# Copying transposed tokens out of PSUM: the order in which the elements of one copy are walked

## The chip, the cores and the metric

The kernel runs on one core of one Trainium2 chip. The metric is the device time of an execution in microseconds (us). In the profile PE is TensorE (PEld its weight loads), DVE is VectorE, ACT is ScalarE, POOL is GpSimd, which here issues the loads. Lnnn is a source line.

## The reference

A sliding-window attention (window 64) feeds a soft mixture of experts.

```python
batch, n_heads, seq, head_dim = (8, 8, 576, 64)      # q, k, v, float32
N, D, E, S_per_e, F = (4608, 512, 8, 4, 1024)        # phi, w1, w2, float32

mask = (rel >= 0) & (rel < 64)
attn = softmax(where(mask, q @ k.T / 8, -1e9))       # per head
x = (attn @ v) as [4608, 512]
logits = x @ phi                                     # 32 slots
slot_input = softmax(logits, over tokens).T @ x
slot_out[e] = relu(slot_input[e] @ w1[e]) @ w2[e]
out = softmax(logits, over slots) @ slot_out
```

## The kernel before

The attention is done in 16 units (8 batches, two halves of four heads each). In a load of q, k or v a partition holds 9 consecutive tokens of one head ("t", T = 9), and the 64 groups of a head ("g") lie on 64 partitions, so that a partition's piece is 9 x 64 elements of one head in a row. The price is that a transpose of one token slice gives columns in the order (h, g) for a single t, and the copy out of PSUM has to put the tokens back into their sequence, where token number = 9 g + t.

```python
def t1(src, dst, on_vector):
    for t0, n in ((0, 5), (5, 4)):
        tr = ps.tile([128, 8, 128], FP16, name="tr", tag="tr")     # PSUM, two buffers
        for j in range(n):
            for x in range(2):
                nc.tensor.transpose(tr[64 * x:64 * x + 64, j, :],
                                    src[:, x, 64 * (t0 + j):64 * (t0 + j) + 64], ident[:, :])
        o = dst.rearrange("p h (g t) -> p t h g", t=T)[:, t0:t0 + n]
        i = tr[:, 0:n, :].rearrange("p t (h g) -> p t h g", h=2)
        if on_vector:
            nc.vector.tensor_copy(out=o, in_=i)      # kT
        else:
            nc.scalar.copy(out=o, in_=i)             # qT, vT

# the order of one unit, cut to the calls (the scheduler moves some of them)
for u in range(nu):
    issue_loads(u)             # q, k, v of unit u + 2, and one weight tile of 1 MB
    for j in range(3):
        stage_t2(u, j)         # transposes windows of vT through "tr", copies to vw (DVE)
        stage_s(u, j)          # scores, exp (ACT), mask (DVE)
        stage_t1(u + 1, j)     # j = 0, 1, 2: t1 of q, k, v of the next unit
        stage_av(*pend)        # attn @ v of the step before, normalised (DVE)
        # ... and one piece of the slot work of a finished batch, also through "tr"
# ... then the experts and the output
```

So each unit has six of these copies: two (5 tokens = 640 elements per partition, 4 tokens = 512) for each of qT and vT on ACT and kT on DVE.

The softmax here doesn't subtract the row's maximum and nothing guards it: scores larger than these inputs give would overflow.

## Time and profile before

| | before |
|---|---|
| time, median of 2 runs | 416.34 us |
| attention stage (16 units of about 21.7 us) | to about 347 us |
| tail (last slot work, experts, output) | about 68 us |
| the six copies, busy time over all units | 252.9 us |

The first lines of the profile's page: busy time and share of the span, then the span in 40 slices of 10.4 us, where a digit is the busy share in tenths, PEclk the granted TensorE clock in tenths, DMA the share of the DMA engines and GB/s what they moved.

```profile
span 414.8 us, 6919 instructions
PE 208.4 (50%) x3028; PEld 152.7 (37%) x3028; DVE 204.5 (49%) x420; ACT 221.8 (53%) x160; POOL 51.7 (12%) x77
...
PEclk9999999999999999999999999999999999889655
DMA  8993997969693979596423324240003300000798
GB/s 110 191 180 49 137 153 105 184 84 184 89 187 48 188 124 177 89 173 112 58 28 43 46 30 57 30 54 5 1 2 53 50 2 2 2 0 2 287 377 246
```

No engine is busy for much over half the time, so the kernel looks like a chain of handoffs. The list of groups by shape shows the copies (count, busy us, mean ns of one, then the idle time before them):

```profile
L143 ACT COPY qT<-tr 128x640 f16<-128x640 f16 x16 | 47.5, 2971 | 15.2 <-PE tr L136 15.2
L143 ACT COPY qT<-tr 128x512 f16<-128x512 f16 x16 | 40.0, 2497 | 0.0
...
L143 ACT COPY vT_103<-tr 128x640 f16<-128x640 f16 x8 | 23.8, 2971 | 43.8 <-PE tr L136 43.8
...
L141 DVE COPY kT_102<-tr 128x640 f16<-128x640 f16 x8 | 23.7, 2961 | 9.9 <-PE tr L136 9.9
...
L167 PEld LDWEIGHTS <-vT_103 128*128 128x128 f16 x144 | 14.8, 137 | 40.8 <-issue 25.5 <-ACT vT_103 L143 14.7
```

A copy takes 2.96 to 2.98 us for 640 elements on both engines: something that they share may set the pace. The timeline shows where such copies stand; the columns are start, duration, engine, line, operation, and in brackets the idle time before it and what ended it. This is one unit, cut to the chain:

```profile
192.55 1.03 PE L167 MATMUL tr<-ident,vT_103 128*128 128x128 f16 x8 [1.50 <-ACT vT_103 L143]
...
194.31 2.98 ACT L143 COPY qT<-tr 128x640 f16<-128x640 f16 x1 [0.78 <-PE tr L136]
...
198.01 2.44 ACT L143 COPY qT<-tr 128x512 f16<-128x512 f16 x1
...
200.50 1.01 PE L167 MATMUL tr<-ident,vT_103 128*128 128x128 f16 x8 [1.69 <-ACT qT L143]
...
202.23 5.22 DVE L141 COPY kT_111<-tr 128x640 f16<-128x640 f16 x2
...
209.23 5.24 ACT L143 COPY vT_112<-tr 128x640 f16<-128x640 f16 x2 [6.41 <-PE tr L136]
...
214.52 1.03 PE L167 MATMUL tr<-ident,vT_112 128*128 128x128 f16 x8 [1.35 <-ACT vT_112 L143]
```

Between the first and the last line lie 22 us, of which the six copies take 15.9: q, then k, then v, with PE waiting for each, because the next transposes need a "tr" buffer that a copy still reads, or the copied tile itself.

### The profile page before, as it was taken

To read this page: it belongs to the slowest core of one execution; us is meant where nothing else is said; L and a number is where in the kernel's file an instruction comes from. 1 tells how busy PE (TensorE), PEld (TensorE's weight loads), DVE (VectorE), ACT (ScalarE), POOL (GpSimd) and SP (SyncE) were. 2 spreads that over 40 slices of the span, in tenths; PEclk is the share of its full clock that TensorE was granted. 3 is DMA by queue.
4 is the path that set the end of the run, shared out by engine and by line. 5 is a ranking of instruction groups with operands and counts; after the bars stand their busy time and mean duration, and the time that the engine had idled before them with its cause. 6 is when DMAs were issued, how large, how long until landed. Compare 5 with 4: busy or idle time off the path is not lost. (4 is left out here: it accounts for less than half of the span.)

```text
span 414.8 us, 6919 instructions
## 1 busy us (share of the span) xinstructions
PE 208.4 (50%) x3028; PEld 152.7 (37%) x3028; DVE 204.5 (49%) x420; ACT 221.8 (53%) x160; POOL 51.7 (12%) x77
## 2 busy tenths in 40 slices
PE   1444445454544545445464544546445455799710
PEld 1333334343433434334344333435334344533100
DVE  0554545546373727273745455464637375511920
ACT  5665666574738291928374665647382916111920
POOL 8311202112121211211001010010001000000000
PEclk9999999999999999999999999999999999889655
DMA  8993997969693979596423324240003300000798
GB/s 110 191 180 49 137 153 105 184 84 184 89 187 48 188 124 177 89 173 112 58 28 43 46 30 57 30 54 5 1 2 53 50 2 2 2 0 2 287 377 246
DMA packets 31069, 40.83 MB, mean 98 GB/s; under 512 B 1856, under 2 KB 22336, under 8 KB 31040
## 3 DMA queue, kind: packets, MB, share of 16 engines
q0 software_dynamic: 26144, 30.97, 49.0%
q1 hardware_dynamic: 4896, 9.44, 6.6%
q8 instruction: 23, 0.38, 0.4%
q14 instruction: 6, 0.05, 0.0%
HBM read 61.93 MB, written 9.44 MB: 172 GB/s over the span
## 5 line engine op out<-in xcount | busy, mean ns | idle before, releaser
L143 ACT COPY qT<-tr 128x640 f16<-128x640 f16 (+1 forms) x32 | 85.5, 2734 | 15.2 <-PE tr L136 15.2
L143 ACT COPY vT_112<-tr 128x640 f16<-128x640 f16 (+1 forms) x16 | 42.0, 2845 | 52.4 <-PE tr L136 52.4
L143 ACT COPY vT_103<-tr 128x640 f16<-128x640 f16 (+1 forms) x16 | 41.9, 2832 | 44.5 <-PE tr L136 44.5
L187 ACT ACTIVATE pm<-sc 128x1024 f16<-128x1024 f32 (+1 forms) x48 | 46.4, 967 | 33.0 <-issue 28.1
L141 DVE COPY kT_102<-tr 128x640 f16<-128x640 f16 (+1 forms) x16 | 41.7, 2794 | 9.9 <-PE tr L136 9.9
L141 DVE COPY kT_111<-tr 128x640 f16<-128x640 f16 (+1 forms) x16 | 41.7, 2790 | 2.2 <-PE tr L136 2.2
L167 PE MATMUL tr<-ident,vT_112 128*128 128x128 f16 x144 | 19.4, 307 | 45.6 <-ACT vT_112 L143 20.8
L169 DVE COPY vw_104<-tr 128x512 f16<-128x512 f16 (+1 forms) x48 | 15.0, 353 | 47.9 <-PE tr L167 47.9
L167 PE MATMUL tr<-ident,vT_103 128*128 128x128 f16 x144 | 19.9, 306 | 37.1 <-ACT vT_103 L143 13.4
L249 PE MATMUL tr<-ident,x_bp 128*128 128x128 f16 x144 | 18.6, 305 | 38.5 <-DVE kT_111 L141 16.6
L191 DVE TENSOR_TENSOR pm<-pm,mask_98 128x512 f16<-128x512 f16 (+1 forms) x96 | 29.8, 349 | 15.7 <-ACT pm L187 15.6
L167 PEld LDWEIGHTS <-vT_112 128*128 128x128 f16 x144 | 14.4, 135 | 48.0 <-issue 25.0
L169 DVE COPY vw_113<-tr 128x512 f16<-128x512 f16 (+1 forms) x48 | 15.2, 352 | 30.0 <-PE tr L167 30.0
L249 PEld LDWEIGHTS <-x_bp 128*128 128x128 f16 x144 | 15.0, 135 | 40.8 <-issue 40.5
L214 PEld LDWEIGHTS <-pm 128*64 128x64 f16 x576 | 28.1, 158 | 4.7 <-issue 2.4
L167 PEld LDWEIGHTS <-vT_103 128*128 128x128 f16 x144 | 14.8, 137 | 40.8 <-issue 25.5
L136 PE MATMUL tr<-ident,qn 128*64 128x128 f16 x288 | 21.3, 313 | 12.5 <-ACT qT L143 7.0
L136 PE MATMUL tr<-ident,vn 128*64 128x128 f16 x288 | 22.2, 311 | 10.6 <-DVE kT_102 L141 2.4
L251 DVE COPY xT<-tr 128x1024 f16<-128x1024 f16 (+1 forms) x20 | 13.7, 686 | 26.6 <-PE tr L249 26.6
L136 PE MATMUL tr<-ident,kn 128*64 128x128 f16 x288 | 21.4, 312 | 7.3 <-ACT qT L143 7.2
L220 DVE RECIPROCAL rc<-av 128x8 f32<-128x8 f32 x32 | 9.2, 287 | 27.0 <-PE av L214 27.0
L222 DVE TENSOR_TENSOR x_bp<-av,rc 128x512 f16<-128x512 f32 x32 | 21.8, 682 | 0.5
(78 smaller groups left out, 323.2 us busy)
## 6 DMA issues: line engine op xcount, KB each, us to landing
out_dram<-ob SPq DMA_DIRECT2D x18, 512.0 KB, 5.5
w1s<-in_moe_w_dram POOLq DMA_DIRECT2D x8, 1024.0 KB, 10.5
w2s<-in_moe_w_dram POOLq DMA_DIRECT2D x7, 1024.0 KB, 10.6
qn<-in_q_dram POOLq DMA_DIRECT2D x16, 288.0 KB, 4.3
kn<-in_k_dram POOLq DMA_DIRECT2D x16, 288.0 KB, 5.1
vn<-in_v_dram POOLq DMA_DIRECT2D x16, 288.0 KB, 5.3
w2l<-in_moe_w_dram POOLq DMA_DIRECT2D x2, 512.0 KB, 7.3
phi_sb<-in_moe_phi_dram POOLq DMA_DIRECT2D x1, 32.0 KB, 5.6
```

Source lines behind the costliest of these rows:

```text
L136: nc.tensor.transpose(tr[64 * x:64 * x + 64, j, :], src[:, x, 64 * (t0 + j):64 * (t0 + j) + 64], ident[:, :])
L141: nc.vector.tensor_copy(out=o, in_=i)
L143: nc.scalar.copy(out=o, in_=i)
L167: nc.tensor.transpose(tr[:, h * n + w, :], st["vT"][:, h, 64 * i:64 * i + 128], ident[:, :])
L169: nc.vector.tensor_copy(out=st["vw"][:, wins[0]:wins[0] + n, h::2, 0:64], in_=tr[:, h * n:h * n + n, :].rearrange("p w (x d) -> p w x d", ...
L187: nc.scalar.activation(pm[:, :, 0:2 * n, :], sc[:, :, 0:128 * n].rearrange("p x (w q) -> p x w q", q=64), AF.Exp, scale=scale)
L191: nc.vector.tensor_tensor(out=pm[:, x, 0:2 * n, :], in0=pm[:, x, 0:2 * n, :], in1=mask0[:, :].unsqueeze(1).broadcast_to([128, 2 * n, 64]), ...
L214: nc.tensor.matmul(av[r0:r0 + 64, kk, 65 * (w // 2):65 * (w // 2) + 65], pm[:, x, h * n + w, :], st["vw"][:, i, kk, 0:65], start=True, sto ...
L220: nc.vector.reciprocal(rc[:, :, :], avv[:, :, :, 64])
L222: nc.vector.tensor_tensor(out=xb[:, c0:c0 + 2, 256 * half:256 * half + 256].rearrange("p c (k d) -> p k c d", d=64), in0=avv[:, :, :, 0:64 ...
L249: nc.tensor.transpose(tr[:, 4 * n + kk, :], xb[:, c, 128 * kk:128 * kk + 128], ident[:, :])
L251: nc.vector.tensor_copy(out=xT[:, 0:4 * len(ch), :], in_=tr[:, 0:4 * len(ch), :])
```

## The change

The intent: let the copy write SBUF in rising order (the tokens of one group innermost) and read PSUM with a stride instead. No instruction is added or removed.

```diff
-            o = dst.rearrange("p h (g t) -> p t h g", t=T)[:, t0:t0 + n]
-            i = tr[:, 0:n, :].rearrange("p t (h g) -> p t h g", h=2)
+            o = dst.rearrange("p h (g t) -> p h g t", t=T)[:, :, :, t0:t0 + n]
+            i = tr[:, 0:n, :].rearrange("p t (h g) -> p h g t", h=2)
```

Before, the write steps 9 elements (18 bytes) and the read is contiguous. After, the write makes runs of 5 (or 4) elements of every 9, and the read steps 128 elements (256 bytes).

## The prediction

> **What bounds the kernel.** No engine is full: the first table has PE at 50%, DVE 49%, ACT 53% of 414.8 us. By the timeline the attention stage (to about 347 us) runs 16 units of 21.7 us, each a chain of handoffs through two PSUM buffers "tr": transposes of v windows (1.0 us), token transposes (0.8), the copies that this change touches, then the next transposes, which wait for a buffer or a copied tile. In the unit from 192.5 to 214.5 us: qT 2.98 + 2.44 on ACT, kT 5.22 on DVE, vT 5.24 on ACT: 15.9 of 22 us, nearly all exposed. The list of waits agrees. From 347 us on, experts and output take 68 us, untouched.
>
> **Why a copy is slow.** A 128x640 copy takes 2.97 us on both engines: 4.3 ns per element after some 0.2 us fixed. It reads contiguously; its write steps 18 bytes[...].[...] plain copies on DVE (xT, 128x1024) take 0.75 us, and the hT cast, which writes runs of 4 contiguous fp16, takes 0.218 us for 64 elements[...]. So 4.3 ns seems to be paid per line, hidden when a line gets four elements.
>
> **What the change does.** Instructions, data and order of work stay. Writes become runs of 5 (or 4) elements, 10 (8) bytes of every 18, in rising order: about 144 lines instead of 640. The read now steps 256 bytes of PSUM.[...] I take reads as nearly free. Estimate for a copy:[...] 0.75 to 1.2, say 1.0 us (0.9 for 512). Six copies cost 5.8 us instead of 15.9.
>
> **On the critical path.** With shorter copies in the timeline's order a unit takes about 12.6 us. That alone would give 416 - 16 x 9.1 = 270 us. A second limit comes up: DMA. In 10 to 160 us its engines are 84 to 89% busy, as nearly all weights load between units 3 and 11. Before unit 12 can be transposed, 26 MB must land; at 157 GB/s (that stretch over its busy share) to 190 (best slices) this takes 138 to 168 us; compute alone needs 152. Sum: about 165 us to unit 12, 58 for the rest, 68 tail.
>
> **Predicted: 290 us, 8 in 10 between 260 and 345.** Faster by over 2%: 0.87; within 2%: 0.08; slower: 0.05.
>
> **What would show it.** Copies qT, kT, vT at 0.75 to 1.2 us in the list of groups; ACT busy falling from 222 to near 110 us, DVE from 205 to near 145; units near 13 us late in the attention stage, longer before; DMA share above 0.95 until about 165 us; transposes waiting for q/k/v loads; the tail unchanged.
>
> **What would make it wrong.** If a strided PSUM read costs like a strided SBUF write, nothing changes.[...] If writes are penalised per 4- or 8-byte word, copies take up to 1.9 us: about 355.

The sum behind the size of a copy came to 0.75 to 1.2 us, entered as 1.0 us for 640 elements and 0.9 for 512, 5.8 us for the six. These sizes, and the total of 291 us built on them (12.6 us a unit; 165 + 58 + 68), are estimates, and so is "reads as nearly free", which no view of the kernel before shows. The 0.2 us fixed is close to what an operation on 4 elements per partition takes on DVE in the trace before (L228, 178 ns). "Line" means 16 bytes of a partition's SBUF: an assumption when this was written, measured later by the first set of copies (write steps of 4, 8 and 9 elements: 1290, 2420 and 2391 ns).

## The result

The kernel after takes 244.97 us (median of 2 runs, 244.91 to 245.03) against 416.34 us; the ratio is 0.588, interval 0.586 to 0.591. Ratios here are the mean time of one kernel's runs over the mean of the other's of the same rounds, so they are not quite the ratio of the quoted medians. The direction was right, the size was not: the time lies below the predicted range of 260 to 345 us.

| | before | after |
|---|---|---|
| time | 416.34 us | 244.97 us |
| six copies, busy time over all units | 252.9 us | 70.2 us |
| ACT busy / DVE busy | 221.8 / 204.5 us | 100.9 / 147.1 us |
| from the start of the slot normalisation (L351) to the end | 54.9 us | 54.1 us |

(The copies' sums are the busy time of lines 141 and 143, without the one table load of 1.3 us on line 143. Adding the groups by shape would give 267.6 and 72.3 us, but the record of a 512 copy often starts before that of the 640 copy has ended, and such time counts once. The last row is the span less the start of that instruction in the chain that ended last, 359.94 and 188.92 us.) The page of the kernel after, slices of 6.1 us:

```profile
span 243.0 us, 6919 instructions
PE 168.3 (69%) x3028; PEld 121.0 (50%) x3028; DVE 147.1 (61%) x420; ACT 100.9 (42%) x160; POOL 51.7 (21%) x77
...
PEclk9999999999996555965756657999996599965555
DMA  5999999999999999999999999006500000079996
GB/s 86 159 192 211 206 207 210 208 209 211 208 212 205 209 208 208 211 206 211 207 209 208 207 206 163 2 3 94 84 3 0 3 0 4 0 270 378 379 374 154
```

Two things are new: the DMA engines are full from the second slice to the 25th (about 150 us), from the fourth to the 24th at 205 to 212 GB/s, and after that they are nearly idle, while attention goes on until 189 us. The groups by shape:

```profile
L143 ACT COPY qT<-tr 128x640 f16<-128x640 f16 x16 | 12.1, 758 | 10.5 <-PE tr L136 10.4
L143 ACT COPY qT<-tr 128x512 f16<-128x512 f16 x16 | 11.8, 735 | 0.0
...
L143 ACT COPY vT_103<-tr 128x640 f16<-128x640 f16 x8 | 6.1, 757 | 25.0 <-PE tr L136 25.0
...
L141 DVE COPY kT_102<-tr 128x640 f16<-128x640 f16 x8 | 6.6, 821 | 7.6 <-PE tr L136 7.4
...
L167 PEld LDWEIGHTS <-vT_103 128*128 128x128 f16 x144 | 11.2, 112 | 6.4 <-ACT vT_103 L143 2.7 <-issue 1.9
```

A copy of 640 now takes 0.76 us on ACT and 0.82 on DVE. The list of waits (us in total, times, longest) has a kind that before had only at the very start:

```profile
PE tr L136 <- DMA vn<-in_v_dram: 17.6, 5, 4.7
...
PEld L136 <- DMA kn<-in_k_dram: 3.7, 5, 1.9
```

And the timeline of one late unit, when the loads are done, cut like the one of before:

```profile
158.01 0.62 PE L167 MATMUL tr<-ident,vT_112 128*128 128x128 f16 x8 [0.17 <-ACT vT_112 L143]
...
159.07 0.76 ACT L143 COPY qT<-tr 128x640 f16<-128x640 f16 x1 [0.22 <-PE tr L136]
...
160.62 0.73 ACT L143 COPY qT<-tr 128x512 f16<-128x512 f16 x1
...
161.41 0.61 PE L167 MATMUL tr<-ident,vT_112 128*128 128x128 f16 x8 [0.33 <-ACT qT L143]
...
162.79 1.45 DVE L141 COPY kT_102<-tr 128x640 f16<-128x640 f16 x2
...
165.37 1.53 ACT L143 COPY vT_103<-tr 128x640 f16<-128x640 f16 x2 [2.26 <-PE tr L136]
```

The vT copies of successive units start at 156.43 and 165.37 us: a unit takes 9 us. Note the first line: eight transposes that took 1.03 us before take 0.62 here, though nothing about them was changed.

### The profile page after: what moved, and what is told of

It reads as the page before. It is cut to its first block, busy times and chain, and to the rows that moved or that the text cites. A ratio compares the mean times of both kernels' runs of the same rounds, so it can differ in the third digit from the quotient of the medians.

```text
span 243.0 us, 6919 instructions
## 1 busy us (share of the span) xinstructions
PE 168.3 (69%) x3028; PEld 121.0 (50%) x3028; DVE 147.1 (61%) x420; ACT 100.9 (42%) x160; POOL 51.7 (21%) x77
## 5 line engine op out<-in xcount | busy, mean ns | idle before, releaser
L187 ACT ACTIVATE pm<-sc 128x1024 f16<-128x1024 f32 (+1 forms) x48 | 39.1, 814 | 25.0 <-issue 18.9
L143 ACT COPY qT<-tr 128x640 f16<-128x640 f16 (+1 forms) x32 | 23.4, 746 | 10.5 <-PE tr L136 10.4
L143 ACT COPY vT_112<-tr 128x640 f16<-128x640 f16 (+1 forms) x16 | 11.8, 739 | 32.3 <-PE tr L136 32.1
L136 PEld LDWEIGHTS <-vn 128*64 128x64 f16 x288 | 12.7, 131 | 21.2 <-DMA vn<-in_v_dram 18.8
L143 ACT COPY vT_103<-tr 128x640 f16<-128x640 f16 (+1 forms) x16 | 11.7, 739 | 27.0 <-PE tr L136 25.5
L61 POOL DMA_DIRECT2D vn<-in_v_dram x16 | 11.4, 715 | 33.0 <-DMA w2s<-in_moe_w_dram 8.4
L167 PE MATMUL tr<-ident,vT_112 128*128 128x128 f16 x144 | 14.7, 251 | 5.2 <-ACT vT_112 L143 2.6
L167 PE MATMUL tr<-ident,vT_103 128*128 128x128 f16 x144 | 15.2, 250 | 3.7 <-ACT vT_103 L143 1.5
L136 PEld LDWEIGHTS <-qn 128*64 128x64 f16 x288 | 11.8, 132 | 10.1 <-DMA qn<-in_q_dram 5.6
L141 DVE COPY kT_102<-tr 128x640 f16<-128x640 f16 (+1 forms) x16 | 11.7, 768 | 7.6 <-PE tr L136 7.4
L61 POOL DMA_DIRECT2D kn<-in_k_dram x16 | 11.4, 714 | 21.1 <-PE tr L136 6.9
L214 PE MATMUL av<-vw_113,pm 128*64 128x65 f16 x288 | 14.3, 216 | 1.3 <-DVE x_bp L229 0.8
```

The costliest lines, as they stand in the source:

```text
L61: nc.gpsimd.dma_start(out=t, in_=src[b, 4 * half:4 * half + 4].rearrange("(x h) (g t) d -> (h g) x (t d)", x=2, h=2, t=T))
L136: nc.tensor.transpose(tr[64 * x:64 * x + 64, j, :], src[:, x, 64 * (t0 + j):64 * (t0 + j) + 64], ident[:, :])
L167: nc.tensor.transpose(tr[:, h * n + w, :], st["vT"][:, h, 64 * i:64 * i + 128], ident[:, :])
L187: nc.scalar.activation(pm[:, :, 0:2 * n, :], sc[:, :, 0:128 * n].rearrange("p x (w q) -> p x w q", q=64), AF.Exp, scale=scale)
L214: nc.tensor.matmul(av[r0:r0 + 64, kk, 65 * (w // 2):65 * (w // 2) + 65], pm[:, x, h * n + w, :], st["vw"][:, i, kk, 0:65], start=True, sto ...
```

## The experiments

My theory after the result had three parts: (1) the copies stand one after the other on the chain, so what each saves shows in the time; (2) a copy is slow because of how its write falls on SBUF, and a strided PSUM read is free; (3) after the change the loads hold the first 150 us. Rivals are named with each run. Times of the kernel before in the same rounds were 415.4 to 416.2 us (medians).

### Half the change: k_only and qv_only

The new order for kT alone (DVE), or for qT and vT alone (ACT):

```diff
+            if on_vector:          # k_only;   qv_only: if not on_vector
                 o = ... "p h g t" ...
+            else:
+                 o = ... "p t h g" ...
```

> Only the kT copies (DVE) get the new order. Chain theory (all six copies of a unit stand one after the other on the chain): saves 5.2 - 1.5 = 3.7 us in each of 16 units, about 59 us, 350 to 360 us. Rival (ACT, the busiest engine, is what bounds, DVE's copies are beside the path): stays within 2% of 416.

> Only the qT and vT copies (ACT) get the new order. Chain theory: saves 10.7 - 3.0 = 7.7 us per unit, 123 us, about 285 to 300 us. Rival (ACT bounds): nearly the whole gain, 245 to 255 us.

k_only took 359.25 us (ratio 0.864, interval 0.862 to 0.866), qv_only 300.35 us (0.722, 0.720 to 0.725). The first is inside the chain theory's range, the second 0.4 us above it. The rival (only ACT bounds) is out: k_only leaves ACT's busy time at 221.7 us and still saves 56 us. The kT copies save 83.4 - 24.1 = 59.3 us of busy time and qT and vT 169.4 - 46.9 = 122.5; the runs saved 56.2 and 115.1, so 95 and 94% of each is exposed. (In k_only PE's window transposes stayed as long as before, 306 ns on average; in qv_only they got shorter, 274 ns, so part of its gain may be PE's.)

### What makes a copy slow: bench, bench2 and bench3

Copies of single forms were appended to the end of the kernel after, each three times on ACT and on DVE, out of a PSUM tile into SBUF. They were single looks of unknown state (349.5, 290.6 and 262.0 us with the added copies); within each form the three copies differ by at most 5 ns, but for one that ranged from 1289 to 1337, and no time of the whole is used. Such a line, with its form (the write takes one element of every 9, the read is contiguous):

```diff
+            eng(out=X[:, 0:4608].rearrange("p (c s) -> p c s", s=9)[:, :, 0], in_=s4)
```

> The kernel after, with copies of single forms appended at its end, three of each on ACT and on DVE (512 or 640 fp16 per partition). Line theory (a write pays about 4.2 ns for every new 16-byte SBUF line, hidden when the line gets 4 or more elements; a strided PSUM read is free): write step 2 elements[...] as cheap as step 1, about 0.6 to 0.7 us; step 4 (2 per line) about 1.3 us; step 8, 9 about 2.4 us; runs of 2 of every 9 about 1.3 us, runs of 4 or 5 about 0.65 to 0.8; strided PSUM read into a contiguous write the same as contiguous to contiguous[...]; from SBUF with write step 9 also about 2.4. Rival 1 (any write whose inner step is not 1 is slow, whatever the line): steps 2 and 4 cost 2.4 us like step 9. Rival 2 (what is slow belongs to reading PSUM in long contiguous runs or to PSUM at all): step 9 from SBUF is fast.

The first set, in the groups by shape (L429 contiguous to contiguous, L433 write step 9, L437 strided read with contiguous write, L439 the form after, L440 the form before, L441 write step 9 from SBUF):

```profile
L440 ACT COPY X<-P 128x640 f16<-128x640 f16 x3 | 8.8, 2949 | 0.1
...
L441 ACT COPY X<-Y 128x512 f16<-128x512 f16 x3 | 7.3, 2422 | 0.1
...
L433 ACT COPY X<-P 128x512 f16<-128x512 f16 x3 | 7.2, 2391 | 0.1
...
L441 DVE COPY X<-Y 128x512 f16<-128x512 f16 x3 | 3.9, 1287 | 0.1
...
L439 ACT COPY X<-P 128x640 f16<-128x640 f16 x3 | 2.3, 752 | 0.1
...
L437 ACT COPY X<-P 128x512 f16<-128x512 f16 x3 | 1.8, 586 | 0.1
```

The strided PSUM read (L437) takes 586 ns, to the nanosecond what contiguous to contiguous takes on ACT (also 586): there it is free. On DVE it takes 691 against 423 ns. Of its strided reads, 640 elements took 825 ns and 512 took 691: 1.05 ns per element and 155 ns fixed. With the same fixed part the contiguous form takes 0.52 ns per element, so DVE is twice as fast there; the change loses that, and it does not matter beside 2.4 us. Rival 2 is out on ACT: from SBUF, step 9 is as slow as from PSUM (2422 and 2391 ns). Rival 1 is out: step 2 took 727 ns and step 4 1290, not 2400. The 16 bytes of a line show as well: from step 4 to step 8 the time rises from 1290 to 2420 ns, and at step 9 it is no longer (2391). But runs of 2 of every 9 took 1090 ns where the line rule wanted 1.3 us, so the rule got a second test.

> More single forms at the end of the kernel after, to test the rule that the first set fitted: time = 0.16 us + the larger of the elements' own rate (0.83 ns on ACT) and 4.4 ns for each time the write enters another 16-byte line. Expected on ACT: step 7, 512 elements: 0.16 + 512 x 14/16 x 4.4 = 2.1 us; step 12, 384 elements: 1.85 us; step 18, 256 elements: 1.29 us; runs of 2 of every 8, 256 runs: 1.29 us (the runs of 2 of every 9 took 1.09, less than the rule's 1.3 to 1.4, so here it may fail); runs of 2 of every 18: 1.29 us; runs of 4 of every 8, 128 lines: 0.73 us. Out of order: single elements put alternately into two contiguous halves: 2.4 us if only one line is kept open, about 0.6 if several are; runs of 4 put alternately into two halves: 0.73 us against 0.6.

```profile
L435 ACT COPY X<-P 128x512 f16<-128x512 f16 x3 | 7.2, 2412 | 0.1
...
L432 ACT COPY X<-P 128x512 f16<-128x512 f16 x3 | 1.8, 607 | 0.1
```

L432 is the runs of 2 of every 8, each in a 16-byte line of its own: 607 ns, not 1290. L435 writes single elements alternately into two contiguous halves: 2412 ns, although each line is filled in the end. The other forms of whole words missed it as well: pairs of every 18 took 612 ns instead of 1290, and runs of 4, of every 8 or in two halves, 586 and 585 instead of 730. So my rule "4.4 ns per new line" failed. What separates the cheap forms (585 to 612 ns) from the dear one (2412) is that a pair that starts at an even element fills one aligned 4-byte word, and a lone fp16 element does not. A third set tested that:

> The second set refuted the rule of 4.4 ns per new line: aligned runs of 2 or 4, each in its own line, cost nothing extra. New rule: what costs 4.4 ns is a lone 2-byte element, half of an aligned 4-byte word, once for each line entered with one; whole words are free wherever they fall. Expected on ACT under it: pairs that start at an odd element, 2 of every 8 (two half words each, 256 lines): 1.29 us; runs of 3 of every 8 (a word and a half, 170 lines): 0.91 us, from an even or an odd start; runs of 4 from an odd start (half, word, half in one line, 128 lines): 0.73 us, where an even start took 0.586; fp32 writes with a step of 16 bytes, 512 elements: 0.59 us (the line rule would say 2.4); fp32 with a step of 36 bytes, 256 elements: 0.37 us.

```profile
L430 ACT COPY X<-P 128x512 f16<-128x512 f16 x3 | 4.0, 1321 | 1.5 <-DVE Y L424 1.5
...
L434 ACT CAST Z<-P 128x512 f32<-128x512 f16 x3 | 3.2, 1057 | 0.0
```

The same pairs, shifted by one element (L430), take 1321 ns instead of 607: whether they fill whole words, not the line alone, decides. Whole words are not quite free, though: fp32 with a step of 16 bytes (L434) took 1057 ns where I expected 590, and fp32 with a step of 36 bytes 612 where I expected 370. That gives a smaller cost for a line entered with whole words only (1.76 ns, below). Put together, on ACT:

time = 161 ns + the larger of 0.83 ns per element and (4.41 ns per line entered with a lone half word + 1.76 ns per line entered with whole words only)

The 0.83 comes from contiguous writes of 640 and 512 elements, (692 - 586) / 128; the 4.41 and 161 from the steps 4 and 8, (2420 - 1290) / 256 and 1290 - 256 x 4.41; the 1.76 from the fp32 step of 36 bytes, (612 - 161) / 256. The rest tests it:

| write form (elements) | lines: half, whole | rule, ns | measured on ACT, ns |
|---|---|---|---|
| step 2 (512) | 128, 0 | 725 | 727 |
| step 7 (512) | 448, 0 | 2137 | 2137 |
| step 12 (384) | 384, 0 | 1854 | 1838 |
| step 18 (256) | 256, 0 | 1290 | 1251 |
| 2 of every 8, even start (512) | 0, 256 | 612 | 607 |
| 2 of every 8, odd start (512) | 256, 0 | 1290 | 1321 |
| 2 of every 9 (512) | 160, 128 | 1092 | 1090 |
| 3 of every 8, even or odd start (510) | 170, 0 | 911 | 911 |
| 4 of every 8, odd start (512) | 128, 0 | 725 | 727 |
| fp32, step 16 bytes (512) | 0, 512 | 1062 | 1057 |
| **before**: step 9, five passes (640) | 640, 0 | 2983 | 2949 |
| **after**: 5 of every 9 (640) | 96, 48 | 692 | 752 |
| **after**: 4 of every 9 (512) | 96, 48 | 669 | 720 |

Step 5 in five passes, also in the first set, fits too (400 lines: 1925 ns, measured 1926). Only the two forms of the kernel after are off by more than 5%: measured, they are slower than the rule by 9 and 8%, and no run shows why. The rule is fitted to this table; what the hardware does in those 4.4 ns no run shows. Where a copy out of PSUM took over 1 us, DVE took the same time as ACT within 3%; from an SBUF source (L441) it took 1287 ns against 2422.

### Do loads hold the kernel after: after_lite and before_lite

The weights of expert 0 alone are loaded and used for all eight experts (wrong results, the same work on the engines):

```diff
-    for e in range(E):
-        w_order += [(load_w1, e), (load_w2, e)]
+    w_order += [(load_w1, 0), (load_w2, 0)]
```

(and the experts read those two tiles; the cap on early weights goes.)

> The kernel after with the weights of expert 0 alone loaded and used for all experts (a wrong result on purpose): 14 MB less to load of 31, same work on the engines. If the loads bound the first 150 us of the kernel after: units run at about 9.2 us throughout, the attention stage ends near 160 instead of 189 us, total 210 to 220 us. Rival (the chain of handoffs still bounds, loads are covered): stays near 245 us.

> Control: the kernel before with the weights of expert 0 alone (wrong on purpose). If loads do not bound the kernel before, although its DMA is 84 to 89% busy in 10 to 160 us: within 1% of 415. If they do: faster by more than 10 us.

Three runs of after_lite took 216.73, 216.90 and 218.90 us (a fourth, slow, 220.06), before_lite 416.07 us (ratio 0.9995, interval 0.998 to 1.001). So loads cost the kernel after about 28 us (244.97 - 216.90, from different rounds) and cost the kernel before nothing, busy as its DMA engines looked. In after_lite the vT copies of twelve successive units start between 37.36 and 136.79 us: 9.04 us per unit throughout.

### A version that beats both: paced and paced_act

The program asks for one weight tile per unit, but weight loads wait for nothing, so the scheduler issued them early: two per unit from unit 5 to 11. Here each is queued behind the v load of its turn; only the order of POOL's loads changes.

```diff
-                f(e)
+                with tc.issue_after(last_load[0].ins): f(e)    # last_load: the v load just issued
```

paced_act also copies kT on ACT instead of DVE.

> The kernel after with each weight load queued behind the v load of its turn, so one weight (1 MB) per unit instead of two between units 5 and 11; nothing else changes in any engine's order. Load theory (the loads of 31 MB at about 208 GB/s are uneven: they hold the early units, while the late units run with idle DMA): a unit then needs 1.9 MB, about 9.2 us, just what its work takes, and the total falls to 217 to 228 us. Rival (total load volume or the chain sets the time, not where the weights stand): within 2% of 245.

> As paced, and the kT copies also go to ACT. In the run with few weights DVE was about 90% busy and ACT half: if DVE now paces a unit, this gains a little over paced, 208 to 222 us. Rival (the handoffs of the chain pace it, or ACT's order with the exps gets in the way): no gain, or up to 10 us slower than paced.

paced took 218.47 us (ratio 0.525, interval 0.521 to 0.528) and paced_act 215.46 us (0.519, 0.517 to 0.522), both correct. That is what after_lite needed, with all weights loaded. paced saves 197.0 us against its before, and the copies got 182.7 us shorter: once the loads are spread, all that the copies save arrives, and 14 us more, for which PE is the candidate (below). What the loads had taken back is 26.5 us (244.97 - 218.47). In paced the DMA engines move 206 GB/s from 12 to 60 us and 208 from 60 to 110: at 208 the 31 MB of loads need about 149 us, so by this estimate the volume of loads would be the next bound. The two intervals touch; the extra 1% of paced_act is small.

The windows of paced hold an experiment that nobody planned. Two stretches, each from one vT copy to the next of a like unit, the same work; the columns are busy us (and instructions) of PE, PEld, DVE, ACT and POOL, then granted clock, DMA share (it counts packets that overlap and can pass 1) and GB/s:

```profile
65.77:75.15 9.38, 7.60 (x178) 5.96 (x176) 8.10 (x24) 5.34 (x10) 2.89 (x4) 1.00 1.23 208
...
102.03:112.61 10.58, 8.83 (x178) 7.14 (x176) 8.27 (x24) 5.47 (x9) 2.89 (x4) 0.84 1.21 206
```

Between 106.9 and 110.3 us PE's bursts took the long times (eight transposes 1.01 and 1.06 us instead of 0.61). Of the 1.2 us by which this unit is longer, 0.2 were lost before, at 103.6 us, where three transposes took 0.55 instead of 0.34 us; the 3.4 us of long bursts cost the other 1.0; the granted clock of the whole stretch was 0.84 instead of 1.00.

The kernel after holds a longer stretch of this kind: a unit with PE's bursts long from its first to its last (eight transposes 1.04 and 1.01 us), in which no engine waits for a load. The first line is that unit (granted clock 0.51), the second the like unit of paced (1.00):

```profile
135.65:146.38 10.73, 9.89 (x176) 7.97 (x174) 7.89 (x23) 5.17 (x8) 2.84 (x4) 0.51 1.21 205
...
75.15:83.92 8.77, 6.81 (x176) 5.53 (x173) 7.82 (x25) 5.19 (x9) 3.02 (x4) 1.00 1.17 209
```

With the same copies, in the same order, a unit with a slow PE takes 2.0 us more.

### Was PE's clock part of the gain: before_sc1 and before_warm

The copies stay slow, and PE gets unused matmuls in its waits. Their output needs a PSUM buffer, so a control gives up one of the two sc buffers first.

```diff
# before_sc1
-        sc = ps.tile([128, 2, 512], FP32, name="sc", tag="sc")
+        sc = ps.tile([128, 2, 512], FP32, name="sc", tag="sc", bufs=1)
# before_warm, in addition, behind each group of token transposes
+            dm = ps.tile([128, 512], FP32, name="dm", tag="dm", bufs=1)
+            for _ in range(3):
+                nc.tensor.matmul(dm[:, :], ones[:, :], dmy[:, :], start=True, stop=True)
```

> Control: the kernel before with one sc buffer instead of two, to free PSUM for the next run. Expected within 2% of before, 410 to 425 us; its transposes of 8 windows still take about 1.0 us.

> The control plus three idle-filling matmuls (128x512, result unused) behind each group of token transposes. Clock theory (part of the gain came because[...] 8 window transposes take 0.61 us instead of 1.03): the bursts get shorter here too, with the slow copies still in place, and a unit saves 1 to 2 us, 380 to 405 us. Rival (copies alone count, PE speed is hidden): within 1.5% of before_sc1, or slower by what the added matmuls take.

(The run asks whether the bursts get shorter when PE's waits are filled; measured until then were only the 0.61 and the 1.03 us.)

before_sc1 took 413.84 us (0.996), as expected. before_warm took 437.13 us (1.052): slower, and outside the 380 to 405 us of the clock theory. The added matmuls were busy for 112.7 us, and the bursts were short only part of the time (eight transposes took 1.04 us in one place and 0.61 in the next). This does not isolate the clock: the means to speed PE up sat on the chain themselves. How much of the 171 us is due to PE's clock stays open; the unplanned stretches in paced and in the kernel after are the only measure.

## Why the prediction was wrong

Right were the chain, the direction and the mechanism in outline: copies at 0.75 to 1.2 us (measured 0.72 to 0.82), ACT near 110 us busy (100.9), DVE near 145 (147.1), a strided PSUM read nearly free (on ACT 586 ns both ways; on DVE 691 against 423), loads becoming a second limit until about 165 us (150), a tail that stays. The prediction's sum was "about 165 us to unit 12, 58 for the rest, 68 tail", 291 us. Measured in the kernel after: the first qT copy of unit 12 starts at 139.3 us, and with the same 68 us for the tail, 243 - 139.3 - 68 = 36 us are left for the rest. So the two first terms were mis-sized, by 26 and 22 us.

1. **"A unit takes about 12.6 us"** is the step that failed most plainly: the 58 us rest on it, and so do the 152 us of compute up to unit 12. After the loads, and throughout after_lite, a unit takes 9.0. Of the 3.6 us, 1.3 are the copies: I took 1.0 and 0.9 us, 5.8 in all, and they measure 0.76 + 0.74 + 0.82 + 0.72 + 0.76 + 0.72 = 4.5. Another 1.0 is a discount: by my own sizes the copies save 10.1 us, and I entered 21.7 - 12.6 = 9.1. The last 1.3 is not in the copies at all: the unit fell by 12.7 us, its copies by 15.9 - 4.5 = 11.4. I kept the durations of PE's bursts from the trace before, but eight transposes fell from 1.03 to 0.62 us and the ten token transposes from 0.74 to 0.47. In the kernel after the ten are short from 19 us on (0.47), and take 0.74 us again at 77.8 us, after a wait of 4.7 us for a load. The granted clock was 1.00 from 19 to 60 us and 0.54 from 77 to 100 us, but it also reads 1.00 where eight transposes took 1.03 us: from 12 to 16 us of the kernel after, and in the unit from 192.5 to 214.5 us of the kernel before. So the column alone does not tell how long a burst is; its measured duration does. I had not asked whether the durations that I carried over would hold. The unit with a slow PE took 2.0 us more in the pair of like units above (10.73 against 8.77), which is enough for the missing 1.3. An estimate from this pair: of the 12.7 us about 2 are PE's and 10.7 the copies', 94% of their 11.4, much the share that k_only showed, where the window transposes stayed at 306 ns. That shorter waits are what made PE fast is not shown: the slow stretch in paced began after a wait of 0.95 us, and in its like unit, after a wait of 0.95 us too, eight transposes took 0.61.

2. **"At 157 GB/s to 190 this takes 138 to 168 us"** was the other. Saturated, the loads run at 207 to 208 GB/s (windows of the kernel after, 12 to 110 us), so that 26 MB take about 125 us. My 157 divided the traffic of 10 to 160 us by the busy share of DMA engines; but engines counted as busy were not always at that rate: slices of before with the same nine tenths move anything from 137 to 191 GB/s. The kernel that the loads hold is the one that shows their rate.

3. **"4.3 ns seems to be paid per line, hidden when a line gets four elements"** gave the right copies by luck, for the wrong reason. In bench2 and bench3 the cost fell on lone half words, once per line (4.41 ns by the rule above); whole words in new lines cost less than half of that (1.76 ns). By the rule the form after is fast (measured 752 ns against 2949) because it enters 144 lines once each, 96 of them with a lone element, where the form before enters a line with a lone element 640 times.

The rivals fell: ACT alone does not bound (k_only), volume of loads alone does not bound the kernel after (paced), and a strided PSUM read costs ACT nothing (bench, 586 ns both ways).

## What to carry to other kernels

When a copy between layouts runs at several nanoseconds per element, and equally slowly on ACT and DVE (here 2.97 us for 640 elements), look at the write: here pairs of 2-byte elements in aligned 4-byte words took 607 ns where the same pairs from an odd start took 1321, and the stride, given to the PSUM read, cost nothing on ACT (586 ns both ways) and 0.27 us on DVE (691 against 423). When a change shortens waits on a chain, do not carry PE durations over from the slow trace without checking whether they hold (here eight transposes took 1.03 us before and 0.62 after), and measure a load rate only where loads are the limit (207 to 208 GB/s here, where I had worked out 157). And after such a gain look at what the freed time runs into: here, putting the weight loads in even order was worth another 26 us.
